# A list scheduler that counts a buffer as free once its store has landed, with another order of the first layer's 29 products

## The chip, the cores and the metric

The kernel runs on one core of one Trainium2 chip. The metric is the device time of one launch in microseconds (us). Before the change it is 998.1 us, the median of three runs.

## What is computed

Sigmoid attention over 8 batches of 12 heads, and then a feed-forward layer with a squared ReLU, all in fp32:

```python
scores = scale * np.matmul(q, k.transpose(0, 1, 3, 2)) - np.log(S)      # q, k, v: (8, 12, 448, 64)
attn = 1.0 / (1.0 + np.exp(-scores))
x = np.matmul(attn, v).transpose(0, 2, 1, 3).reshape(3584, 768)
h = x @ w_in                                                            # 768 -> 2048
r = np.maximum(h, 0.0)
return (s * (r * r) + b) @ w_out                                        # 2048 -> 768
```

## The kernel before

**Stages.** Attention (24 steps) writes x to DRAM. The first 512 of the 3584 tokens then go through the feed-forward layer plainly (the *plain* stage, which the first layer follows at 378.5 us): 16 blocks f, each with a first product into a PSUM tile `ph`, an activation chain r, r*r, s*r+b and a split g on ScalarE and VectorE, and a second product into `po`. The other 3072 tokens go in two groups of three blocks of 512. Each group runs a first layer of 29 products (`LAYERS[0]`: a fast scheme in place of 36 block products) and a second of 15. A product r of the first layer runs as two *units* of 12 matmuls, p = 0 and 1; the first layer of a group has 58 units.

**Precision.** Each fp32 operand is split in two fp32r parts: hi is a copy on ScalarE, lo is the difference on VectorE. An operand `s_14_0l` is the lo part of product 14's operand in group 0, `a_21` a raw block of x, `a_t`, `a_o` sums of such blocks, `h_...` a PSUM bank pair with a product, `G...` a sum of products in SBUF. An entry of `SUMS` for the weights is made on VectorE as `t_f_g` (f is the quarter of the weights, g the group of rows), split, and stored to the DRAM tensors `wd`, from which each unit fetches its 512 KB of weights as `wu`. The sums for later quarters (`t_e`, `t_r`, `t_y`, `t_p`, `t_u`) are made during the first layer.

**Order.** From the plain stage on, each engine's order is made by the list scheduler `Flow.run` (lines 213 to 254) at build time. It takes, of all operations that are able to run, the one with the earliest planned start, and then the earliest due time; PE's order is fixed by `seq`. A transfer out is an SP operation with cost 0.1 and a lag (5 to 9) that counts for those who read what it wrote. The engines run their orders strictly from front to back, SP too: an instruction that waits holds up all behind it. SP's transfers take eight completion semaphores in turn, so a transfer is issued only when the eighth before it has landed.

**Buffers.** `Slots` (line 504) hands out named buffers, the one that was freed first coming first. In the plain stage 13 buffers of 6 KB per partition (c0 to c7, t0 to t4, the list `cx`) hold the weights and the sums `t_f_g`; a sum's buffer is given back in the same step that issues its store, and the next tile in it waits on the chip until that store has landed. The two layers use the list `heap` with buffers of 4 KB. When all of the plain stage is planned, `end` closes its pools and gives `heap` 34 more buffers l0, l1, ..., which lie where c0, c1, ... lay: l0 and the first half of l1 in c0, l4 across c2 and c3. A tile in such a buffer waits for the last use of what lay there, its store included. In the kernel before, c3 is last used by `t_3_5` and c0 by `t_3_0`; l0 goes to `s_23_0l`, and l4 to the fourth tile after it, the sum t10 (`a_t_3838`).

**PSUM.** Four bank pairs take the units in turn. A unit that starts or continues a chain in a pair waits until the sum of the product before it has been read by VectorE or ScalarE.

Of the kernel before, what the change touches and what calls it, by code (L numbers as in the profile page):

```python
# [118 lines left out]
         28: ("o28", "t8", 1)},  # L119
        chains=((14, 5, 25, 0), (4,), (23, 27, 18), (12,), (10, 11, 7, 9, 8), (2,), (22, 16),  # L120
         (15, 3, 19, 24), (13, 17, 28, 21, 1, 26), (20,), (6,)),
        seq=((20, 1), (23, 0), (14, 1), (27, 0), (5, 1), (18, 0), (25, 1), (12, 0), (0, 1), (2, 0),
         (15, 1), (10, 0), (3, 1), (11, 0), (19, 1), (7, 0), (24, 1), (9, 0), (13, 1), (8, 0),
         (17, 1), (22, 0), (28, 1), (16, 0), (21, 1), (4, 0), (1, 1), (6, 0), (26, 1)),
        accs={"00": (("S19", 1), ("S26", 1), ("S3", -1), ("S8", -1)),
         "01": (("S13", 1), ("S19", -1), ("S4", 1)),
         "02": (("S1", 1), ("S10", -1)),
# [36 lines left out]
        seq=((8, 0), (13, 1), (6, 0), (10, 1), (7, 0), (1, 2), (2, 3), (3, 0), (5, 2), (4, 3), (11, 1),  # L164
         (12, 3), (14, 0), (0, 1), (9, 0)),
# [14 lines left out]
    ),  # L180
)

ON_VECTOR = (("13", 1),)
FIRST_RAW = ("20", "11", "12", "21", "22", "10", "00", "02", "01")


class Op:
# [11 lines left out]
class Flow:  # L199
# [13 lines left out]
    def run(self, free):  # L213
        tensor = [o for o in self.ops if o.eng == "PE"]
        t = 0.0
        for o in tensor:
            t += o.cost
            o.due = t
        for o in reversed(self.ops):
            for x, whole in o.next:  # L220
                o.due = min(o.due, x.due - x.cost - (o.lag if whole else -o.cost))
        free = {"PE": 0.0, "DVE": 0.0, "ACT": 0.0, "SP": 0.0, **free}
        able = {e: [o for o in self.ops if o.eng == e and not o.wait] for e in free}
        tensor = tensor[::-1]
        left = len(self.ops)
        while left:
            best = None
            point = tensor[-1].due if tensor else 1e9
            for e, at in free.items():
                for o in able[e]:  # L230
                    if e == "PE" and o is not tensor[-1]:
                        continue
                    need = o.need()
                    if need:
                        far = o.due - o.cost - o.lag - point
                        if far > o.ahead or need + o.heap.spare * (far > self.FAR) > len(o.heap.free_):
                            continue
                    key = (max(at, o.ready), o.due)
                    if best is None or key < best[0]:
                        best = (key, o)  # L240
            (start, _), o = best
            if o.eng == "PE":
                tensor.pop()
            able[o.eng].remove(o)
            o.fn()
            free[o.eng] = start + o.cost
            o.end = start + o.cost + o.lag
            left -= 1
            for x, whole in o.next:
                x.wait -= 1  # L250
                x.ready = max(x.ready, o.end + self.LATENCY if whole else start)
                if not x.wait:
                    able[x.eng].append(x)
        return free
# [213 lines left out]
def sigmoid_attention_relu2_ffn(  # L468
# [11 lines left out]
    B, NQ, P, _, _, S = qk.shape  # L480
    D = v.shape[5]
    NF, _, DM = w_in.shape
# [20 lines left out]

    class Slots:


        def __init__(self, pl, n, tag, ahead=1e9, spare=0):
            self.free_ = [(pl, f"{tag}{i}") for i in range(n)]
            self.at = {}
            self.ahead, self.spare = ahead, spare  # L510

        def more(self, pl, n, tag):
            self.free_ += [(pl, f"{tag}{i}") for i in range(n)]

        def tile(self, shape, dtype, name):
            pl, tag = self.free_.pop(0)
            t = pl.tile(shape, dtype, tag=tag, name=name)
            self.at[id(t)] = (t, pl, tag)
            return t

        def free(self, t):
            _, pl, tag = self.at.pop(id(t))
            self.free_.append((pl, tag))

    heap = Slots(pool(ctx, "h0", 1), 1, "g", 24.0, 4)
    first = ExitStack()
# [22 lines left out]
    def f32(ap):  # L549
        return ap.bitcast(F32)  # L550
# [166 lines left out]
    at = ExitStack()  # L717
# [326 lines left out]
    flow = Flow(heap)  # L1044
# [6 lines left out]
    class Emit:  # L1051
# [101 lines left out]
        def out(self, net, n, k, v):  # L1153
            m, c = self.block[k]
            v.uses += 1
            v.stored = True

            def fn():
                out_store(f32(v.t), KC * c, threes[n][m], KC)
                net.drop(v)  # L1160

            flow.op("SP", 0.1, fn, (v.by,))

        units = []

        def matmuls(self, flow, cost, fn, after, n, l, r, p):
            x = len(self.units)
            rows = made.get((l, p, LAYERS[l]["operand"][r][0]), [])
            old = self.units[x - ROLL] if x >= ROLL else None
            w = flow.op("SP", 0.1, fetch, [old, *rows], lag=5.0, behind=self.ready)  # L1170
            self.ready = [w]
            first = [self.evicted[x - 1]] if 0 < x < 4 else []
            u = flow.op("PE", cost, fn, [w, *after, *first], behind=[self.switch])
            self.units.append(u)
            if 5 <= x < 8:

                def store():
                    out_store(f32(outs[x - 5]), 2 * (x - 5), 0, 2)
                    spare.free(outs[x - 5])
                    heap.free_.append(spare.free_.pop())  # L1180

                flow.op("SP", 0.1, store, (u,))
            return u

    em = Emit()
# [12 lines left out]
    def finish(n, k, p, v, sign):  # L1198
# [3 lines left out]
        s = sign * v.sign  # L1202
        if (k, p) in ON_VECTOR:
            v.by = flow.op(
# [104 lines left out]
    def out_store(src, e, t, n):  # L1309
        dst = out[e * P : (e + n) * P, t * TB : (t + 1) * TB]  # L1310
        nc.sync.dma_start(dst.rearrange("(c p) t -> p c t", p=P), src)
# [265 lines left out]
```

## Time and profile before

| | |
|---|---|
| median of three runs | 998.1 us (997.24, 998.1, 1000.76) |
| the profiled execution's own time | 997.09 us |
| its span | 995.3 us |
| PE busy | 984.9 us (99%) |
| VectorE (DVE) busy | 853.2 us (86%) |
| ScalarE (ACT) busy | 704.0 us (71%) |
| mean DMA rate over the span | 283 GB/s |

The span is the time from the first to the last instruction of one profiled execution; the execution's own time is 1.8 us longer. PE is busy nearly throughout, so what can be won on it is in its few waits, and what can be lost is any new wait. The stages have different limits, and each is read from its own window.

### The profile page before, as it was taken

The numbers are of one execution on the slowest core, as the hardware profiler recorded it, in microseconds if no ns is written. First come the engines' busy times: TensorE is split into PE (matmuls) and PEld (weight loads), VectorE is DVE, ScalarE is ACT, GpSimd is POOL, SyncE is SP. The second block draws the span as 40 slices with busy tenths as digits, with TensorE's granted clock in tenths as the row PEclk, the third lists the DMA queues.
The fourth block names the chain that finished last, engine by engine and source line by source line (L and its number), as shares of the span: only waits on it lengthen the run. The fifth ranks groups of instructions, "written<-read, shape, count | busy, mean of one in ns | idle before, by whom it ended". The sixth has DMA issues, their size and how long they took to land.

```text
span 995.3 us, 13889 instructions
## 1 busy us (share of the span) xinstructions
PE 984.9 (99%) x5240; PEld 774.9 (78%) x5240; DVE 853.2 (86%) x939; ACT 704.0 (71%) x768; POOL 0.2 (0%) x4
## 2 busy tenths in 40 slices
PE   9999999999999989999999999999999999999998
PEld 4545555554888878887888888888888888888887
DVE  5999999997899787998999999975786789999932
ACT  7999999998777566557899945522447799955500
POOL 0000000000000000000000000000000000000000
PEclk9999999999999999999999999999999999999999
DMA  9788989996688999987887677899766676777773
GB/s 328 281 329 345 352 334 370 361 383 249 242 324 346 373 403 399 400 326 272 321 280 231 204 223 252 242 326 318 236 208 199 204 207 197 207 222 247 227 239 123
DMA packets 100210, 281.94 MB, mean 283 GB/s; under 512 B 10160, under 2 KB 20528, under 8 KB 100144
## 3 DMA queue, kind: packets, MB, share of 16 engines
q1 hardware_dynamic: 99856, 280.59, 81.8%
q8 instruction: 42, 0.69, 0.3%
q10 hardware_dynamic: 288, 0.46, 0.1%
q14 instruction: 24, 0.20, 0.0%
HBM read 196.08 MB, written 84.93 MB: 282 GB/s over the span
## 4 chain that ended last, share of the span: by engine, by line
PE 60%; DVE 6%; DMA 3%; ACT 1%; issue 1%; SPq 0%; DVEq 0%; ACTq 0%
PE o L1107 31%; PE h L1107 28%; DVE t L568 2%; DVE w L568 1%; DMA wd<-t 1%; DVE t L565 1%; DMA wd<-t_u 1%; DVE g L568 1%; PE po L1317 1%; DMA a<-xd 1%; ACT s_0h L1086 0%; DMA wu<-wd 0%; SPq L710 0%; PE o L1124 0%; DVE G L565 0%
## 5 line engine op out<-in xcount | busy, mean ns | idle before, releaser
L1107 PE MATMUL h<-s_0h,wu 128*128 128x512 f32 x928 | 276.6, 379 | 1.8 <-DVE G L565 1.8
L1107 PEld LDWEIGHTS h<-s_0h,wu 128*128 128x128 f32 x928 | 175.4, 189 | 27.1 <-DVE G L565 2.2
L1107 PE MATMUL h<-s_0l,wu 128*128 128x512 f32 x464 | 175.9, 379 | 0.0
L773 ACT ACTIVATE a<-psc,nls 128x896 f32<-128x896 f32 x144 | 132.0, 1016 | 10.9 <-PE psc L793 8.7
L827 PE MATMUL pav<-a,v 128*64 128x448 f32 x576 | 113.8, 543 | 1.4
L1107 PEld LDWEIGHTS h<-s_0l,wu 128*128 128x128 f32 x464 | 87.7, 189 | 12.5
L827 PEld LDWEIGHTS pav<-a,v 128*64 128x64 f32 x576 | 39.1, 137 | 65.7 <-issue 45.3
L1200 ACT ACTIVATE G<-G 128x1024 f32<-128x1024 f32 x68 | 69.9, 1049 | 10.0 <-DVE G L565 9.8
L1107 PE MATMUL o<-g_0h,wu 128*128 128x512 f32 x240 | 76.3, 379 | 0.0
L1107 PE MATMUL o<-g_1h,wu 128*128 128x512 f32 x240 | 76.3, 379 | 0.0
L1107 PE MATMUL o<-g_2h,wu 128*128 128x512 f32 x240 | 76.3, 379 | 0.0
L1107 PE MATMUL o<-g_3h,wu 128*128 128x512 f32 x232 | 73.7, 379 | 0.0
L1317 PE MATMUL po<-g,w 128*128 128x512 f32 x288 | 66.9, 387 | 3.1 <-ACT g L1452 2.9
L1317 PEld LDWEIGHTS po<-g,w 128*128 128x128 f32 x288 | 55.5, 193 | 12.3 <-ACT g L1452 3.3
L1080 ACT COPY G<-h 128x1024 f32<-128x1024 f32 x36 | 36.4, 1012 | 36.0 <-PE h L1107 22.3
L936 PE MATMUL ph<-x0h,w 128*128 128x512 f32 x192 | 59.5, 380 | 0.0
L793 PE MATMUL psc<-qkh 64*128 64x448 f32 x282 | 53.8, 378 | 0.0
L565 DVE TENSOR_TENSOR G<-G,h 128x1024 f32<-128x1024 f32 x40 | 48.1, 1213 | 3.8 <-PE h L1107 3.8
L1107 PEld LDWEIGHTS o<-g_0h,wu 128*128 128x128 f32 x240 | 45.4, 189 | 6.5
L1107 PEld LDWEIGHTS o<-g_1h,wu 128*128 128x128 f32 x240 | 45.4, 189 | 6.5
L1107 PEld LDWEIGHTS o<-g_2h,wu 128*128 128x128 f32 x240 | 45.4, 189 | 6.5
L568 DVE TENSOR_TENSOR qkl<-qk,qkh 128x1664 fp32r<-128x1664 f32 (+3 forms) x26 | 44.9, 1726 | 6.3 <-ACT qkh L756 6.1
(222 smaller groups left out, 1978.9 us busy)
## 6 DMA issues: line engine op xcount, KB each, us to landing
wu<-wd SPq DMA_DIRECT2D x236, 512.0 KB, 4.3
wd<-t SPq DMA_DIRECT2D x40, 768.0 KB, 6.3
qk<-qk_t SPq DMA_DIRECT2D x23, 896.0 KB, 7.3
st<-w_out SPq DMA_DIRECT2D x16, 768.0 KB, 9.7
st<-w_in SPq DMA_DIRECT2D x16, 768.0 KB, 8.8
v<-v_t SPq DMA_DIRECT2D x24, 448.0 KB, 5.7
xd<-xo SPq DMA_DIRECT2D x24, 448.0 KB, 4.9
wd<-w SPq DMA_DIRECT2D x16, 512.0 KB, 5.1
```

Of the source, the lines that this page charges most:

```text
L565: nc.vector.tensor_tensor(o, x, y, op=ALU.add)
L568: nc.vector.tensor_tensor(o, x, y, op=ALU.subtract)
L773: nc.scalar.activation(a, psc[:, :, :S], AF.Sigmoid, bias=nls, scale=SCALE)
L793: nc.tensor.matmul(o[:, j, :S], two[wi][r, i, cols], paired(two[xi][r, i, :S]), start=m == 0, stop=m == 2,)
L827: nc.tensor.matmul(pav[r, i, :S], ld_[1][:, 3 * i + c, j, :], a[i, c][:, j, :], start=c == 0, stop=False,)
L936: nc.tensor.matmul(ph, w[:, k, wi, kc * P : (kc + 1) * P], paired(x0[h][xi][:, cc, :]), start=m == 0, stop=m == 3 * NCC - 1,)
L1080: nc.scalar.copy(o, self.view(x, l))
L1107: nc.tensor.matmul(bank.t[0][:, j], wt[:, w, wi, x * P : (x + 1) * P], paired((o.hi, o.lo)[xi][:, c, :]), start=new and m == 0, stop=stop ...
L1200: v.by = flow.op("ACT", cost, lambda: nc.scalar.activation(f32(v.t), f32(v.t), *a, **kw), (v.by,))
L1317: nc.tensor.matmul(pos[e], w[:, k, wi, kc * P : (kc + 1) * P], paired(g[:, gi, :]), start=first and i == 0, stop=last and i == 2,)
```

## The change

The scheduler's planned start now includes the time at which the buffers that an operation would take come free (`Slots.ready`), and a buffer given back by an operation comes free at that operation's planned end with its lag (`Slots.now`). The two kinds of output stores get lags of 8 and 9. The buffers that `more` adds come with the free time 0. The first layer's units run in another order; which products are chained in a bank is as before. Two more of the 24 squared ReLUs of a group go from two ScalarE instructions to one VectorE instruction: three in place of one. `FIRST_RAW` is read nowhere.

```diff
-        seq=((20, 1), (23, 0), (14, 1), (27, 0), (5, 1), (18, 0), (25, 1), (12, 0), (0, 1), (2, 0),
...
+        seq=((12, 1), (14, 0), (23, 1), (5, 0), (27, 1), (25, 0), (18, 1), (0, 0), (20, 1), (15, 0),
...
-ON_VECTOR = (("13", 1),)
+ON_VECTOR = (("01", 0), ("12", 0), ("20", 0))
...
-                    key = (max(at, o.ready), o.due)
+                    key = (max(at, o.ready, o.heap.ready(need)), o.due)
                     if best is None or key < best[0]:
                         best = (key, o)
             (start, _), o = best
             if o.eng == "PE":
                 tensor.pop()
             able[o.eng].remove(o)
+            free[o.eng] = start + o.cost
+            type(o.heap).now = o.end = start + o.cost + o.lag
             o.fn()
-            free[o.eng] = start + o.cost
-            o.end = start + o.cost + o.lag
...
     class Slots:
 
+        now = 0.0
 
         def __init__(self, pl, n, tag, ahead=1e9, spare=0):
-            self.free_ = [(pl, f"{tag}{i}") for i in range(n)]
+            self.free_ = [(pl, f"{tag}{i}", 0.0) for i in range(n)]
...
         def more(self, pl, n, tag):
-            self.free_ += [(pl, f"{tag}{i}") for i in range(n)]
+            self.free_ += [(pl, f"{tag}{i}", 0.0) for i in range(n)]
+
+        def ready(self, n):
+            return max((x[2] for x in self.free_[:n]), default=0.0)
 
         def tile(self, shape, dtype, name):
-            pl, tag = self.free_.pop(0)
+            pl, tag, _ = self.free_.pop(0)
...
         def free(self, t):
             _, pl, tag = self.at.pop(id(t))
-            self.free_.append((pl, tag))
+            self.free_.append((pl, tag, self.now))
...
-            flow.op("SP", 0.1, fn, (v.by,))
+            flow.op("SP", 0.1, fn, (v.by,), lag=8.0)
...
-                flow.op("SP", 0.1, store, (u,))
+                flow.op("SP", 0.1, store, (u,), lag=9.0)
```

What this moves on VectorE where `t_3_2` takes its buffer, late in the plain stage. Before (the buffer is that of `t_2_6`, whose lo part is the first row):

```order
L568 TENSOR_TENSOR t_2_6_3436<-t_2_6_3436 128x3x256
L565 TENSOR_TENSOR t_3_0_3463<-wf_15_2682 128x256
L568 TENSOR_TENSOR t_3_0_3463<-wf_7_2681,t_3_0_3463 128x256
L568 TENSOR_TENSOR t_3_0_3463<-t_3_0_3463 128x256
L568 TENSOR_TENSOR w_6_3519<-wf_6_125,w_6_3519 128x3x256
L568 TENSOR_TENSOR t_2_3_3374<-t_2_3_3374 128x3x256
L568 TENSOR_TENSOR t_2_4_3400<-t_2_4_3400 128x3x256
L568 TENSOR_TENSOR t_3_1_3537<-wf_3_114,wf_11_116 128x256
L568 TENSOR_TENSOR t_3_2_3561<-wf_3_114,wf_11_116 128x256
```

On the same engine and at the same place, now (the buffer of `t_3_2` is that of `t_2_3`, whose lo part stands six rows ahead of the first row):

```order
L572 TENSOR_TENSOR g_3463<-r_3428,g_3463 128x512
L572 TENSOR_TENSOR t_2_6_3471<-wf_6_126,wf_10_112 128x256
L572 TENSOR_TENSOR w_7_3466<-wf_7_2681,w_7_3466 128x3x256
L569 TENSOR_TENSOR t_2_6_3471<-wf_10_112 128x256
L569 TENSOR_TENSOR t_2_6_3471<-wf_2_110 128x256
L572 TENSOR_TENSOR t_2_5_3438<-t_2_5_3438 128x3x256
L572 TENSOR_TENSOR w_6_3517<-wf_6_125,w_6_3517 128x3x256
L572 TENSOR_TENSOR t_3_0_3524<-wf_7_2681,wf_15_2682 128x256
L572 TENSOR_TENSOR t_2_6_3471<-t_2_6_3471 128x3x256
L572 TENSOR_TENSOR t_3_1_3530<-wf_3_114,wf_11_116 128x256
L572 TENSOR_TENSOR t_3_2_3533<-wf_3_114,wf_11_116 128x256
```

The new tile stood seven VectorE instructions behind the one whose store it waits for; it now stands fifteen behind.

VectorE at the end of the plain stage and the start of the first layer, before (`g` is the last activation split, after which `s_23_0l` takes l0):

```order
L568 TENSOR_TENSOR t_3_5_3670<-t_3_5_3670 128x3x256
L568 TENSOR_TENSOR g_3746<-r_3731,g_3746 128x512
L568 TENSOR_TENSOR s_23_0l<-a_o_3735,s_23_0h 128x1024
L568 TENSOR_TENSOR a_t_3832<-a_11_3478,a_21_3486 128x1024
L568 TENSOR_TENSOR a_t_3834<-a_20_3475,a_22_3521 128x1024
L568 TENSOR_TENSOR a_t_3836<-a_12_3481,a_t_3832 128x1024
L565 TENSOR_TENSOR a_t_3838<-a_t_3836,a_t_3834 128x1024
L568 TENSOR_TENSOR a_o_3840<-a_22_3521,a_t_3836 128x1024
L565 TENSOR_TENSOR a_t_3834<-a_21_3486,a_t_3834 128x1024
L568 TENSOR_TENSOR s_14_0l<-a_21_3486,s_14_0h 128x1024
```

The same place now:

```order
L572 TENSOR_TENSOR t_3_5_3673<-t_3_5_3673 128x3x256
L572 TENSOR_TENSOR g_3751<-r_3743,g_3751 128x512
L572 TENSOR_TENSOR s_14_0l<-a_21_3487,s_14_0h 128x1024
L572 TENSOR_TENSOR a_o_3833<-a_11_3492,a_12_3495 128x1024
L572 TENSOR_TENSOR a_t_3835<-a_11_3492,a_21_3487 128x1024
L572 TENSOR_TENSOR a_t_3837<-a_20_3557,a_22_3705 128x1024
L572 TENSOR_TENSOR a_t_3839<-a_12_3495,a_t_3835 128x1024
L569 TENSOR_TENSOR a_t_3841<-a_t_3839,a_t_3837 128x1024
L572 TENSOR_TENSOR a_o_3843<-a_22_3705,a_t_3839 128x1024
L569 TENSOR_TENSOR a_t_3837<-a_21_3487,a_t_3837 128x1024
L572 TENSOR_TENSOR s_23_0l<-a_o_3833,s_23_0h 128x1024
```

Product 14 is now the second product (units 2 and 3) and 23 the third (units 4 and 5). `s_14_0l` takes l0, the first tile after the plain stage; in the changed plan c0, where l0 lies, is last used by `t_3_5`.

SP's queue at the same place, before (`wd<-` rows are stores of weight sums and weights, `wu` fetches for units; the program's first fetch for a unit and five raw blocks stand further ahead):

```order
L698 DMA wd_3_96<-w_7_3631 128x2x512
L698 DMA wd_3_96<-w_15_3660 128x3x512
L1427 DMA wd_1_92<-t_3_0_3463 128x3x512
L1427 DMA wd_1_92<-t_3_6_3674 128x3x512
L1038 DMA wu_0_20_1_3729<-wd_1_92 128x1024
L1038 DMA wu_0_23_0_3733<-wd_0_91 128x1024
L1427 DMA wd_1_92<-t_3_3_3597 128x3x512
L1427 DMA wd_1_92<-t_3_4_3636 128x3x512
L1427 DMA wd_1_92<-t_3_5_3670 128x3x512
```

SP's queue now (two fetches for units and five raw blocks, a_10 among them, stand further ahead; the sixth, a_22, is here):

```order
L1042 DMA wu_0_14_0_3661<-wd_0_91 128x1024
L1042 DMA wu_0_14_1_3665<-wd_1_92 128x1024
L1042 DMA wu_0_23_0_3668<-wd_0_91 128x1024
L1431 DMA wd_1_92<-t_3_0_3524 128x3x512
L1431 DMA wd_1_92<-t_3_2_3533 128x3x512
L714 DMA a_22_3705<-xd_86 128x2x256
L714 DMA a_22_3705<-xd_87 128x2x256
L1431 DMA wd_1_92<-t_3_4_3630 128x3x512
L702 DMA wd_3_96<-w_15_3709 128x3x512
L1431 DMA wd_1_92<-t_3_6_3677 128x3x512
L1431 DMA wd_1_92<-t_3_3_3595 128x3x512
L1431 DMA wd_1_92<-t_3_5_3673 128x3x512
```

Ahead of the last store of the plain stage, that of `t_3_5`, there are now five fetches for units where there were three, and six raw blocks where there were five; all stores are as many as before.

## Rows read from the trace of the kernel before

**Rows 1.** The waits of PE over the whole span (engine, line, what it waited for: us in total, times, longest).

```profile
PE po L1317 <- ACT g L1452: 2.9, 1, 2.9
PE h L1107 <- DVE G L565: 1.8, 1, 1.8
```

**Rows 2.** The timeline of PE at the end of the plain stage (start us, us, line, operation, out<-in, count; in brackets the idle time before it and its releaser).

```profile
361.23 8.25 PE L1317 MATMUL po<-g,w 128*128 128x512 f32 x36
372.33 0.48 PE L1317 MATMUL po<-g,w 128*128 128x512 f32 x1 [2.85 <-ACT g L1452]
373.06 5.62 PE L1317 MATMUL po<-g,w 128*128 128x512 f32 x17 [0.24 <-DVE g L568]
378.52 0.38 PE L1107 MATMUL h<-s_0h,wu 128*128 128x512 f32 x1
```

**Rows 3.** Busy time of each engine in stretches of the span (PE, PEld, DVE, ACT, POOL, each with its count; then the granted clock as a share of 2.4 GHz, the DMA share and GB/s).

```profile
373.00:378.70 5.70, 5.64 (x18) 4.69 (x19) 4.54 (x5) 2.93 (x5) 0.00 (x0) 0.70 0.99 363
378.70:433.00 54.30, 54.30 (x253) 47.54 (x253) 49.45 (x54) 30.47 (x35) 0.00 (x0) 1.00 1.04 405
458.00:531.00 73.00, 72.80 (x337) 63.79 (x338) 69.39 (x76) 64.37 (x69) 0.00 (x0) 1.00 0.83 283
```

**Rows 4.** The timeline of VectorE around its longest wait in the plain stage, and below it two of the waits in the stretch 283 to 470 us.

```profile
341.18 0.42 DVE L568 TENSOR_TENSOR t<-wf,wf 128x256 f32<-128x256 f32 x1
350.27 0.43 DVE L568 TENSOR_TENSOR t<-wf,wf 128x256 f32<-128x256 f32 x1 [8.67 <-DMA wd<-t]
369.75 1.82 DVE L568 TENSOR_TENSOR t<-t 128x768 fp32r<-128x768 f32 x2
...
DVE w L568 <- ACT w L682: 1.8, 1, 1.8
ACT w L682 <- DMA wd<-t: 1.8, 1, 1.8
```

**Rows 5.** The timeline of ScalarE at the end of the last activation chain.

```profile
366.90 0.59 ACT L1448 ACTIVATE r<-ph 128x512 f32<-128x512 f32 x1
...
369.87 1.04 ACT L1086 CAST s_0h<-a_o 128x1024 fp32r<-128x1024 f32 x1 [1.71 <-DVE a_o L568]
...
371.66 0.62 ACT L1452 CAST g<-r 128x512 fp32r<-128x512 f32 x1
```

**Rows 6.** The timeline of VectorE at the start of the first layer; the row at 386.40 is `s_14_0l`.

```profile
376.32 1.22 DVE L568 TENSOR_TENSOR a_t<-a,a_t 128x1024 f32<-128x1024 f32 x1
382.99 1.23 DVE L565 TENSOR_TENSOR a_t<-a_t,a_t 128x1024 f32<-128x1024 f32 x1 [5.45 <-DMA wd<-t]
...
386.40 1.22 DVE L568 TENSOR_TENSOR s_0l<-a,s_0h 128x1024 fp32r<-128x1024 f32 x1
```

**Rows 7.** The last three stores of the plain stage, those of `t_3_3`, `t_3_4` and `t_3_5`: the transfers of `wd` issued in two short stretches (count, ns of the issue, first and last start), with their times from issue to landing.

```profile
L1427 SPq DMA_DIRECT2D wd<-t x2: 371/410/450, 369.9 to 370.7; - x2
DMA to landing us min/median/max: 9.1/9.9/10.6
...
L1427 SPq DMA_DIRECT2D wd<-t x1: 360/360/360, 371.6 to 371.6; - x1
DMA to landing us min/median/max: 11.3/11.3/11.3
```

**Rows 8.** Stretches of the span with the columns of rows 3, from the start of the heavy storing to the landing of the last store.

```profile
285.00:309.00 24.00, 24.00 (x112) 21.00 (x112) 23.97 (x46) 18.44 (x28) 0.00 (x0) 1.00 1.05 408
309.00:315.00 6.00, 6.00 (x29) 5.27 (x28) 4.20 (x10) 4.23 (x7) 0.00 (x0) 1.00 0.93 357
315.00:320.00 5.00, 5.00 (x24) 4.37 (x24) 5.00 (x11) 3.95 (x7) 0.00 (x0) 1.00 0.42 163
320.00:335.00 15.00, 15.00 (x71) 13.14 (x70) 14.86 (x30) 10.96 (x18) 0.00 (x0) 1.00 1.05 408
335.00:346.00 11.00, 11.00 (x53) 9.63 (x52) 6.60 (x11) 6.75 (x11) 0.00 (x0) 1.00 1.01 329
...
350.00:370.00 20.00, 19.43 (x89) 16.36 (x87) 19.73 (x36) 14.87 (x22) 0.00 (x0) 1.00 1.05 407
370.00:375.00 5.00, 2.43 (x6) 1.77 (x7) 4.26 (x5) 2.83 (x4) 0.00 (x0) 0.82 0.98 343
375.00:383.00 8.00, 8.00 (x35) 6.86 (x34) 2.55 (x4) 3.88 (x6) 0.00 (x0) 0.90 1.05 413
```

**Rows 9.** DMA issues of the whole span (out<-in, queue, count, KB each, median us from issue to landing).

```profile
wu<-wd SPq DMA_DIRECT2D x236, 512.0 KB, 4.3
wd<-t SPq DMA_DIRECT2D x40, 768.0 KB, 6.3
```

**Rows 10.** The timelines of VectorE and of PE at PE's other wait.

```profile
451.07 1.22 DVE L568 TENSOR_TENSOR s_0l<-a,s_0h 128x1024 fp32r<-128x1024 f32 x1
455.18 0.69 DVE L568 TENSOR_TENSOR t_e<-wr 128x512 f32<-128x512 f32 x1 [2.89 <-DMA wd<-t_u]
...
458.20 0.48 PE L1107 MATMUL h<-s_0h,wu 128*128 128x512 f32 x1 [1.82 <-DVE G L565]
```

**Rows 11.** The squared ReLU on either engine: the instructions of line 1206, and a group of the page's part 5.

```profile
L1206 DVE SCALAR_TENSOR_TENSOR G<-G x2: 1211/1214/1218, 545.1 to 822.4; 128x1024 f32<-128x1024 f32 x2
...
L1200 ACT ACTIVATE G<-G 128x1024 f32<-128x1024 f32 x68 | 69.9, 1049 | 10.0 <-DVE G L565 9.8
```

More of the change, by code (lines that the diff above doesn't have):

```diff
@@ L121 @@
          (15, 3, 19, 24), (13, 17, 28, 21, 1, 26), (20,), (6,)),
-        seq=((20, 1), (23, 0), (14, 1), (27, 0), (5, 1), (18, 0), (25, 1), (12, 0), (0, 1), (2, 0),
-         (15, 1), (10, 0), (3, 1), (11, 0), (19, 1), (7, 0), (24, 1), (9, 0), (13, 1), (8, 0),
-         (17, 1), (22, 0), (28, 1), (16, 0), (21, 1), (4, 0), (1, 1), (6, 0), (26, 1)),
+        seq=((12, 1), (14, 0), (23, 1), (5, 0), (27, 1), (25, 0), (18, 1), (0, 0), (20, 1), (15, 0),
+         (22, 1), (3, 0), (16, 1), (19, 0), (4, 1), (24, 0), (2, 1), (10, 0), (13, 1), (11, 0),
+         (17, 1), (7, 0), (28, 1), (9, 0), (21, 1), (8, 0), (1, 1), (6, 0), (26, 1)),
         accs={"00": (("S19", 1), ("S26", 1), ("S3", -1), ("S8", -1)),
@@ L181 @@
 )
-ON_VECTOR = (("13", 1),)
-FIRST_RAW = ("20", "11", "12", "21", "22", "10", "00", "02", "01")
+ON_VECTOR = (("01", 0), ("12", 0), ("20", 0))
+FIRST_RAW = ("10", "21", "11", "12", "20", "22", "01", "02", "00")
 class Op:
```

## The prediction

> **What bounds the kernel now.** I read first the waits of PE over the whole span. There are two that matter: 2.9 us for the last activation split, and 1.8 us for a sum on VectorE [rows 1]. PE does the same matmuls after the change, so a gain can come from these two places alone, and a loss only from a new wait.
>
> The timeline shows the first place. PE ends 36 matmuls at 361.23 + 8.25 = 369.48, waits 2.85, then 0.24, and the remaining 17 take 5.62 at a granted clock of 0.70 on average, so partly at 1.2 GHz [rows 2, 3]. At full clock 253 matmuls start in 54.30 us, 0.215 each [rows 3]; the last 18 would have ended 18 x 0.215 = 3.9 after 369.3, and the first layer would start at 373.2, not at 378.52 [rows 2]. This place costs 5.3 us.
>
> Its cause is on VectorE: nothing runs for 8.67 us, behind a store's landing [rows 4], and the order shows why: `t_3_2` takes the buffer of `t_2_6` seven instructions after the latter's last use. ScalarE's chain then ends late, held up once more by 1.71 [rows 5]. The second place is of one kind with it: `t_e` waits 2.89 for the landing of `t_u`'s store, and the sum that PE needs stands behind it; PE loses 1.82 [rows 10].
>
> **The change, part by part.** *The planned waits.* Both cases are what the new key sees. `t_3_2` now stands 15 instructions behind its store. Without the 8.67 us, the last `t` lo ends not at 371.6 [rows 4] but near 363; the last split cannot come before the last `ph` at 361.2 plus four ScalarE steps and one on VectorE, some 365 to 367 (two such steps take 0.6 each, [rows 5]), still ahead of 369.3. So PE would reach the first layer at 373.2: -5.3 us there. `t_e` should lose its wait too: -1.8 us.
>
> *What is late next.* I follow l0. `s_14_0l`, needed by unit 2, now takes l0, which lies in c0; c0's last user is now `t_3_5`, whose store is the last of the plain stage. Buffers from `more` have free time 0, so the plan does not know of this wait. Before, the same wait fell on l4 (the 5.45 at 382.99, [rows 6]), when `s_23_0l` and three sums were already done. Call the landing of that store R. Before: issued 371.6, 11.3 later landed, R = 382.9 [rows 7], as VectorE's restart at 382.99 shows.
>
> R is set by the DMA, not by VectorE. From 285 us on the DMA share is 1.05 at 407 or 408 GB/s in all stretches but 309 to 320, 335 to 346 (share 1.01, raw blocks moving at 329) and 370 to 375 [rows 8]. All that SP issues ahead of the last store must pass first. Now there are two more unit fetches and one more raw block ahead, 3 x 512 KB (a fetch in [rows 9]; a raw block is 128 x 1024 fp32, the same size): 1.57 MB / 408 GB/s = 3.9 us. Raw blocks are slower: (408 - 329) GB/s x 11 us = 0.87 MB lost over the five of them, 0.4 us for one. Sum 4.3. Against it, gaps that can close: 309 to 315, (408 - 357) x 6 = 0.31 MB, 0.7 us; 315 to 320, 245 x 5 = 1.2 MB, 3.0 us; 370 to 375, 0.8 us [rows 8]. The first two follow a wait of the removed kind (ScalarE's split waits 1.8 for a store, VectorE 1.8 for the split, [rows 4]); I count them as closed. R = 382.9 + 4.3 - 3.7 = 383.5; bounds 382.7 (all closed) and 387.2 (none).
>
> Then PE: units 0 and 1 run from 373.2 to 373.2 + 24 x 0.215 = 378.4. Unit 2 waits for `s_14_0l`, R + 1.1 = 384.6: a new wait of 6 us. Unit 4 needs `s_23_0l`, ninth on VectorE after R; one instruction takes (386.40 - 382.99) / 3 = 1.14 [rows 6], so R + 10.3 = 393.8, a second new wait of 2 to 4 us. Before, unit 4 began at 378.52 + 48 x 0.215 = 388.8. So the hand-over comes out at 393.8 - 388.8 = +5.0 us, not -5.3. Before, 17 matmuls after a wait of 2.85 took 5.62, where 3.7 were due: 1.9 for the clock [rows 2, 3]. After unit 2's wait this is covered, since unit 4 waits anyway; after unit 4's it costs 0 to 1.9. The wait of 1.82 [rows 10] stands in no low clock. I take 1.0.
>
> *VectorE for ScalarE.* Four more VectorE instructions of 1.21 in all, eight fewer of 1.05 on ScalarE [rows 11]: 2.4 us on VectorE in each group's first layer. Between 458 and 531 VectorE has 73.0 - 69.4 = 3.6 us free [rows 3], which hides it; uncovered it costs 2.4. No gain: PE waits for ScalarE nowhere but at the hand-over. I take 0.
>
> *The order of products* has no price of its own beyond what it puts in l0. New lags of output stores only affect later buffer choice: 0.
>
> Sum: +5.0 + 1.0 - 1.8 = +4.2 us on 997.1, so 1001.3. The median of the runs lies 1.0 above the profiled execution; 1002 on that basis, +0.4%. 0.5% (5 us) is about what a measurement of this kernel can tell from no change, so this counts as no change, near the edge.
>
> **The rivals.** *The gain arrives.* If R does not wait for all that stands ahead, both PE waits go and nothing replaces them: -5.3 - 1.8 = -7.1, 991. With a landing of 6.3, the median of such stores [rows 9], after an issue at 364 to 366, R is 370 to 372, earlier than unit 2 can ask. It breaks even (clock apart) at R + 10.3 = 388.8 + 1.8, R = 380.3. Against it: the last three stores took 9.1, 10.6 and 11.3, each landing behind the one before [rows 7], and the DMA has no room [rows 8]. The Trainium skill says otherwise in principle: its page "DMA: Bandwidth & Descriptors", section "Queues, rings and completion order", says that completion is not first-in, first-out per issuing engine. By that rule the last store could overtake and this rival would hold, 991; the order of the landings above does not bear it out.
>
> *Slower.* The gaps do not close, since VectorE now waits elsewhere for the crowded DMA: R = 387.2, unit 4 at 397.5, +8.7; the full 1.9 for the clock; -1.8: +8.8, 1006 to 1007. The total is R - 380.3 plus the clock's part: it passes 5 us at R = 385.3 with none of it and at 383.4 with all. For it: SP issues raw blocks in a burst, and the store of `t_2_5` stands behind eight such transfers. Against: the cause of the biggest gap is gone.
>
> *It does not do what it says.* The plan's SP steps cost 0.1 and landings vary from 4 to 11, so waits of the old kind come back and the stall before the hand-over stays in part; with the wait on l0 behind it, that is 1000 +- 3, since R, not the stall, then sets the start.
>
> **How the numbers follow.** Forecast 0.52, of which 0.12 ends above +5 us by the clock; gain 0.13, of which 0.01 ends within 5 us; slower 0.28; no effect 0.07. Faster: 0.12. Slower: 0.28 + 0.12 = 0.40. Within: 0.40 + 0.01 + 0.07 = 0.48. Range: from 995, which leaves out most of the gain case, to 1008, above the slower one; the forecast's own range is 998 to 1006.
>
> **What would show it.** Right: the wait for ACT g at `po` is gone and the first matmul of the first layer starts near 373; PE waits some 6 us on VectorE one product later, and again before the third; VectorE waits on `wd<-t` right before its first 128x1024 split after the last g; the DMA gap at 315 to 320 is filled; no wait of `t_e` on `t_u`. The forecast is wrong if VectorE restarts before 380 (faster) or after 385 (slower), or if a PE wait stands after the first ten units.

## The result, and the profile after

| | before | after |
|---|---|---|
| median of six runs | 997.67 us (996.74 to 1000.76) | 1003.48 us (1002.96 to 1004.39) |
| profiled execution, own time and span | 997.09, 995.3 us | 1003.71, 1001.9 us |

After over before: 1.0055, 95% interval 1.004 to 1.007. The waits of PE over the span, after:

```profile
PE h L1111 <- DVE s_0l L572: 8.0, 2, 5.9
PE h L1111 <- DVE a_t L569: 1.1, 1, 1.1
...
PE h L1111 <- DMA wu<-wd: 0.3, 1, 0.3
```

Both waits of [rows 1] are gone; two waits for `s_0l` and two small ones took their place. PE's timeline shows where:

```profile
361.59 11.82 PE L1321 MATMUL po<-g,w 128*128 128x512 f32 x54
...
384.68 0.79 PE L1111 MATMUL h<-s_0l,wu 128*128 128x512 f32 x1 [5.88 <-DVE s_0l L572]
...
393.89 0.48 PE L1111 MATMUL h<-s_0l,wu 128*128 128x512 f32 x1 [2.09 <-DVE s_0l L572]
...
424.45 0.45 PE L1111 MATMUL h<-s_0h,wu 128*128 128x512 f32 x1 [0.33 <-DMA wu<-wd]
...
428.35 0.45 PE L1111 MATMUL h<-s_0h,wu 128*128 128x512 f32 x1 [1.07 <-DVE a_t L569]
```

The 54 matmuls of the plain stage now run without the stall of [rows 2]. PE then stops ahead of unit 2 and of unit 4. VectorE's timeline gives the reason:

```profile
365.62 0.69 DVE L572 TENSOR_TENSOR g<-r,g 128x512 fp32r<-128x512 f32 x1 [0.72 <-ACT g L1456]
383.40 1.22 DVE L572 TENSOR_TENSOR s_0l<-a,s_0h 128x1024 fp32r<-128x1024 f32 x1 [17.09 <-DMA wd<-t]
...
392.62 1.22 DVE L572 TENSOR_TENSOR s_0l<-a_o,s_0h 128x1024 fp32r<-128x1024 f32 x1
...
427.14 1.22 DVE L569 TENSOR_TENSOR a_t<-a,a_t 128x1024 f32<-128x1024 f32 x1 [5.04 <-DMA a<-xd]
```

`s_14_0l` stands 17.09 us behind the landing of a store. In [rows 6] a wait of this kind was 5.45 us, and the operands that PE took first were ahead of it. Stretches of the span (columns of [rows 3]):

```profile
309.00:315.00 6.00, 6.00 (x30) 5.26 (x29) 6.00 (x13) 4.29 (x7) 0.00 (x0) 1.00 1.05 404
315.00:320.00 5.00, 5.00 (x25) 4.39 (x24) 5.00 (x12) 4.93 (x8) 0.00 (x0) 1.00 1.05 406
320.00:335.00 15.00, 15.00 (x71) 13.16 (x70) 13.92 (x25) 10.93 (x17) 0.00 (x0) 1.00 0.95 370
...
370.00:375.00 5.00, 5.00 (x25) 4.38 (x24) 0.00 (x0) 3.52 (x6) 0.00 (x0) 1.00 1.06 402
...
393.90:400.00 6.10, 6.10 (x20) 5.07 (x21) 6.10 (x6) 4.88 (x7) 0.00 (x0) 0.72 0.28 80
```

The DMA gaps of [rows 8] at 309 to 320 and at 370 are filled; a smaller one has opened at 320 to 335. Behind unit 4's wait 20 matmuls take 6.10 us where 20 x 0.215 = 4.3 were due, at a mean granted clock of 0.72: 1.8 us.

Added up: unit 4 at 393.89 against 388.8 is +5.1, the clock +1.8, the waits at 424 and 428 +1.4, the wait of [rows 10] -1.8. That is +6.5; the spans differ by 6.6. The clock's 1.8 and the wait of 0.33 at 424.45 are one item, not two: in the runs l0_last and old_relu below, which have the same hand-over, no low clock followed unit 4 (28 matmuls in about 6.1 us, at 1.00), and PE then waited 1.97 and 1.76 for the same weights, up to 424.47 and 424.34. So about 2 us are lost up to 424 with the low clock or without it, and the landing of those weights sets them.

### The profile page after: what moved, and what is told of

The parts are those of the page before. It is cut to its first block, busy times and chain, and to the rows that moved or that the text cites. A ratio compares the mean times of both kernels' runs of the same rounds, so it can differ in the third digit from the quotient of the medians.

```text
span 1001.9 us, 13890 instructions
## 1 busy us (share of the span) xinstructions
PE 987.1 (99%) x5240; PEld 777.0 (78%) x5240; DVE 857.9 (86%) x943; ACT 692.2 (69%) x756; POOL 0.2 (0%) x4
## 4 chain that ended last, share of the span: by engine, by line
PE 80%; ACT 8%; DMA 5%; DVE 3%; issue 2%; SPq 1%; ACTq 0%; DVEq 0%
PE o L1111 31%; PE h L1111 27%; PE pav L831 9%; ACT a L777 5%; PE ph L940 4%; PE po L1321 3%; DMA wd<-t 2%; PE psc_l L818 2%; PE pav L840 2%; PE psc L797 2%; DMA a<-xd 1%; DVE t L572 1%; DMA out_t<-o 1%; ACT wf L597 1%; DMA wu<-wd 1%
## 5 line engine op out<-in xcount | busy, mean ns | idle before, releaser
L1111 PE MATMUL h<-s_0h,wu 128*128 128x512 f32 x928 | 279.5, 382 | 1.4 <-DVE a_t L569 1.1
L1204 ACT ACTIVATE G<-G 128x1024 f32<-128x1024 f32 x66 | 67.6, 1048 | 27.3 <-DVE G L569 27.0
L1321 PE MATMUL po<-g,w 128*128 128x512 f32 x288 | 64.4, 379 | 0.0
L1084 ACT COPY G<-h 128x1024 f32<-128x1024 f32 x32 | 32.0, 1010 | 32.8 <-PE h L1111 20.8
```

Source lines behind the costliest of these rows:

```text
L1084: nc.scalar.copy(o, self.view(x, l))
L1111: nc.tensor.matmul(bank.t[0][:, j], wt[:, w, wi, x * P : (x + 1) * P], paired((o.hi, o.lo)[xi][:, c, :]), start=new and m == 0, stop=stop ...
L1204: v.by = flow.op("ACT", cost, lambda: nc.scalar.activation(f32(v.t), f32(v.t), *a, **kw), (v.by,))
L1321: nc.tensor.matmul(pos[e], w[:, k, wi, kc * P : (kc + 1) * P], paired(g[:, gi, :]), start=first and i == 0, stop=last and i == 2,)
```

## The experiments

All are compared with the kernel before, timed beside each. The theory was that the loss is where `s_14_0l` lies: in c0, behind the last store. The main rival was that the three more transfers ahead of the hand-over are the loss, whatever waits for them.

**1. l0_last.** Hand out l0 and l1 last, by name.

```diff
             heap.more(pool(ctx, "h2", 1), 34, "l")
+            heap.free_.sort(key=lambda x: x[1] in ("l0", "l1"))
```

> Edit: the changed kernel, with the buffers l0 and l1 (those that lie in c0, which t_3_5 leaves last) put at the end of the list that `more` adds; every engine's order stays as it is, only addresses move. Buffer theory (the loss is that s_14_0l stands behind the landing of t_3_5's store, R = 383.4): VectorE's wait of 17.1 us goes, PE enters the first layer at 373.2 and unit 2 follows without the 5.9 us, unit 4 without the 2.1 us; the first layer is up to 388.8 - 383.6 = 5.3 us earlier than in the kernel before, and the 1.8 us of t_e stay away: 991, or up to 995 if unit weights, which come behind R, are late for units 5 to 7 (due 386 to 391). DMA theory (the three more transfers ahead of the hand-over are the loss, whatever waits for them): the wait moves to the unit weights or the raw block a_22, and the time stays within 2 us of 1003.5.

Measured: 1004.83 us, ratio 1.0086 (1.0069 to 1.0103), VectorE at 383.38 as in the changed kernel. It decides nothing on the theory: a name gets its address at its first use, so `s_14_0l` took l2 and the address was c0 again. It repeats the changed kernel.

**2. c0_last.** The same, but l0 and l1 get their addresses first, by a tile each (`place_0`, `place_1`) that nobody uses, and are then handed out last. The instruction orders are those of the changed kernel.

```diff
-            heap.more(pool(ctx, "h2", 1), 34, "l")
+            pl = pool(ctx, "h2", 1)
+            for i in range(2):
+                pl.tile([P, 2, TB], F32, tag=f"l{i}", name=f"place_{i}")
+            heap.more(pl, 34, "l")
+            heap.free_ = heap.free_[2:] + heap.free_[:2]
```

> Edit: the changed kernel, but the addresses of l0 and l1 (the two buffers in c0) are set aside first and the two are handed out last; every engine's order is that of the changed kernel. s_14_0l now takes a buffer whose last reader is PE, done at 361. Buffer theory: VectorE goes on at 366 without the wait of 17.1 us, waits for the raw block a_22 (near 374) instead, and has s_23_0l near 381; unit 2 and unit 4 follow without a wait, from 373.2 on, 10.3 us ahead of the changed kernel and 5.2 ahead of the kernel before, with no low clock behind a wait: 990 to 993, or up to 996 if the weights of units 5 to 7 (due 386 to 391) are late. DMA theory: the wait moves to the weights or to a_22, and the time stays above 1000.

Measured: 993.15 us (992.82 to 993.66), ratio 0.9955 (0.994 to 0.997): faster than both kernels. VectorE and PE:

```profile
366.27 1.22 DVE L572 TENSOR_TENSOR s_0l<-a,s_0h 128x1024 fp32r<-128x1024 f32 x1
...
373.75 1.23 DVE L572 TENSOR_TENSOR a_t<-a,a 128x1024 f32<-128x1024 f32 x1 [3.99 <-DMA a<-xd]
...
379.56 1.22 DVE L572 TENSOR_TENSOR s_0l<-a_o,s_0h 128x1024 fp32r<-128x1024 f32 x1
```

```profile
413.53 0.45 PE L1111 MATMUL h<-s_0h,wu 128*128 128x512 f32 x1 [1.29 <-DMA wu<-wd]
417.44 0.45 PE L1111 MATMUL h<-s_0h,wu 128*128 128x512 f32 x1 [1.08 <-DVE a_t L569]
```

The raw block a_22 is the next to be late, as expected, and costs PE nothing. PE has no wait from 361 to 413 and so no low clock. The span is 10.9 us shorter than after: 10.3 at unit 4 and 1.8 of clock, less 1.0 at the weights (11.1 by this sum). Measured at the end of the wait for weights it is 424.45 - 413.53 = 10.9. The rival falls.

**3. fetch_late and twice.** These test the bytes ahead of the last store: three fetches behind it, or two more transfers ahead of it. `em.tail` collects the stores of the last quarter.

```diff
-            w = flow.op("SP", 0.1, fetch, [old, *rows], lag=5.0, behind=self.ready)
+            w = flow.op("SP", 0.1, fetch, [old, *rows], lag=5.0, behind=self.ready + (self.tail if x == 2 else []))
...
+                if f == 3:
+                    em.tail.append(o)
```

```diff
+                    if f == 3 and g in (3, 4):
+                        x = dram.tile([P, len(rows) * 2 * KW], F32, name=f"twice_{g}")
+                        nc.sync.dma_start(x, f32(box[0]).rearrange("p k h c -> p (k h c)"))
                     stored.update((0, f, n) for n in rows)
```

> Edit: the changed kernel with the fetches of weights for units 2 to 4 (3 x 512 KB) held behind the last store of the plain stage; t_3_5 still leaves c0 last and s_14_0l still takes l0. The term of the prediction (R falls by 1.57 MB / 408 GB/s = 3.9 us): VectorE restarts at 379.5 instead of 383.4, unit 4 starts at 389.8 instead of 393.9, and the time falls by 4: 999 to 1000, if the weights of unit 2, now 1.3 us behind R, are not much later than s_14_0l. Rival (R hangs on VectorE, ScalarE or on when SP issues the last store, not on the bytes ahead of it): R stays above 382 and the time at 1002 to 1005.

> Edit: the changed kernel with two more transfers of 768 KB out of the buffers of t_3_4 and t_3_3 to a scratch tensor, ahead of the last store (1.57 MB that nobody reads). By the same term R rises by 3.9 us to 387.3, unit 4 starts at 397.8 and the time rises by 3.9 to 1007.5, by 3.4 to 5 with the clock. Rival (the landing hangs on something else): 1003 to 1005.

Measured: fetch_late 999.71 us, ratio 1.0027 (1.0016 to 1.0038); twice 1007.71, ratio 1.0103 (1.0086 to 1.012). `s_14_0l` on VectorE and unit 4 on PE, first of fetch_late, then of twice:

```profile
379.14 1.22 DVE L572 TENSOR_TENSOR s_0l<-a,s_0h 128x1024 fp32r<-128x1024 f32 x1 [13.37 <-DMA wd<-t]
...
389.63 0.48 PE L1111 MATMUL h<-s_0l,wu 128*128 128x512 f32 x1 [2.19 <-DVE s_0l L572]
```

```profile
388.54 1.22 DVE L572 TENSOR_TENSOR s_0l<-a,s_0h 128x1024 fp32r<-128x1024 f32 x1 [21.49 <-DMA wd<-t]
...
399.03 0.48 PE L1111 MATMUL h<-s_0l,wu 128*128 128x512 f32 x1 [1.36 <-DVE s_0l L572]
```

R moves by -4.3 and +5.1 where 3.9 were due, unit 4 with it by -4.3 and +5.1, and the medians by -3.8 and +4.2. The term holds in size, within 0.4 and 1.2 us. In twice the plain stage's last g on VectorE starts 0.7 later than after (366.36 against 365.62), in fetch_late 0.5 earlier (365.08). That these shifts make up the difference is not shown: in l0_last that g starts 0.8 earlier (364.79), and R stays at 383.38.

What the bytes move is the issue of the last store. The last stores on SP's queue, of fetch_late, after and twice in turn (ns of the issue, first and last start, then the times to landing):

```profile
L1431 SPq DMA_DIRECT2D wd<-t x2: 1097/1367/1637, 365.3 to 366.5; - x2
DMA to landing us min/median/max: 11.6/12.0/12.5
L1431 SPq DMA_DIRECT2D wd<-t x1: 1852/1852/1852, 371.4 to 371.4; - x1
DMA to landing us min/median/max: 11.9/11.9/11.9
L1431 SPq DMA_DIRECT2D wd<-t x1: 770/770/770, 376.5 to 376.5; - x1
DMA to landing us min/median/max: 11.9/11.9/11.9
```

The last store goes out at 366.5, 371.4 and 376.5 and lands 12.5, 11.9 and 11.9 later. So the time behind the issue stays nearly the same, and the added bytes hold up the queue ahead of it.

**4. sched_alone and order_alone.** Each half of the change by itself (the old order with the new scheduler; the new order with the old scheduler). The choice of squared ReLUs goes with the order.

```diff
-        seq=((12, 1), (14, 0), (23, 1), (5, 0), (27, 1), (25, 0), (18, 1), (0, 0), (20, 1), (15, 0),
...
+        seq=((20, 1), (23, 0), (14, 1), (27, 0), (5, 1), (18, 0), (25, 1), (12, 0), (0, 1), (2, 0),
...
-ON_VECTOR = (("01", 0), ("12", 0), ("20", 0))
+ON_VECTOR = (("13", 1),)
```

This is sched_alone, from the changed kernel; order_alone is the reverse edit of the kernel before.

> Edit: the changed kernel with the old order of the products and the old choice of squared ReLUs; the scheduler's new key and the lags stay. Here c0 is last used by w_7, whose store stands far ahead of the last; t_3_5 lies in c7, under l10 and l11 (a raw block and s_14_0h). Buffer theory: the stall before the hand-over goes (-5.3 us), t_e's wait too (-1.8 us), and the first operands after the hand-over wait for no late store; third product's hi needs t_3_5's landing near 380, its unit is due at 383.6, so 0 to 2 us of new wait, and up to 3 us if the weights of the fourth unit, fetched behind t_3_5's store, are late: 991 to 996, faster than the kernel before. Rival (a plan that waits for landings is itself the loss, since it moves fetches ahead of stores): 1001 to 1004.

> Edit: the kernel before with the new order of the products and the new choice of squared ReLUs; the scheduler is the old one. c0 is now last used by t_3_2, whose store stands three stores (5.8 us of DMA time) ahead of that of t_3_5; VectorE's order at the hand-over is that of the changed kernel. Buffer theory: VectorE restarts near 377.6, unit 2 waits 0.4 to 1 us, unit 4 starts near 388 in place of 388.8 before: with 0 to 1.9 us for the clock and 0 to -1.8 us for t_e the time is 995 to 999. Rival (the order of the products is the loss, since it sets the fetches ahead of the stores): 1002 to 1005, as the changed kernel.

Measured: sched_alone 998.39 us, ratio 1.0008 (0.9999 to 1.0018); order_alone 1000.88, ratio 1.0042 (1.0027 to 1.0057). Both missed their ranges by 2 us, for reasons beyond the hand-over. There both did as expected: sched_alone has no wait of PE up to 447, and in order_alone VectorE and PE show

```profile
376.61 1.23 DVE L568 TENSOR_TENSOR s_0l<-a,s_0h 128x1024 fp32r<-128x1024 f32 x1 [8.98 <-DMA wd<-t]
```

```profile
361.27 11.82 PE L1317 MATMUL po<-g,w 128*128 128x512 f32 x54
372.92 0.38 PE L1107 MATMUL h<-s_0h,wu 128*128 128x512 f32 x1
...
387.10 0.52 PE L1107 MATMUL h<-s_0l,wu 128*128 128x512 f32 x1 [2.19 <-DVE s_0l L568]
...
418.99 0.45 PE L1107 MATMUL h<-s_0h,wu 128*128 128x512 f32 x1 [1.66 <-DMA wu<-wd]
```

so unit 4 starts 1.7 us earlier than before (388.8). The first two rows of PE show more: with the old scheduler the stall ahead of the hand-over is gone as well (VectorE's longest wait for a store in the plain stage is 3.44 us here, 8.67 before), and so is the wait at 458. The new order is enough for that, as the new scheduler is in sched_alone. The later waits (1.66, and 2.6 from 487 to 521) and the clock behind unit 4 (in the stretch 384.7 to 393.9, 25 matmuls take 7.00 us, 1.6 too long) give back more: -1.7 - 1.8 + 1.66 + 2.6 + 1.6 = +2.4, of the 3.4 by which the spans differ; 1.0 stays unexplained. In sched_alone one wait at 452 takes the whole gain:

```profile
452.14 0.79 PE L1111 MATMUL h<-s_0h,wu 128*128 128x512 f32 x1 [5.04 <-ACT G L1084]
```

```profile
430.00:458.00 28.00, 22.89 (x94) 18.85 (x93) 19.96 (x21) 20.56 (x22) 0.00 (x0) 0.88 0.71 250
```

The second row is its stretch 430 to 458: beside the 5.04, 94 matmuls take 22.89 where 20.2 were due, 2.7 for the clock. 7.7 lost against 7.1 gained is 998.

**5. order_late_last and before_c3_last.** The edit of c0_last (with 12 addresses given out first) with the buffers in c0 and c3 on order_alone, and with those in c3 alone (l4, l5) on the kernel before.

```diff
+            heap.free_.sort(key=lambda x: x[1] in ("l0", "l1", "l4", "l5"))
```

> Edit: the run order_alone with the buffers that lie in c0 and c3 (l0, l1, l4 and l5; t_3_2 and t_3_4 leave them last) handed out last; every order stays. Buffer theory: VectorE's wait of 9.0 us goes, and with it PE's waits of 1.0 and 2.2 us at 384 and 387 and the 1.7 us of half clock behind them: 1000.9 - 4.9 = 996, 993.5 to 997.5 with the waits that stay (1.7 us for weights at 419, four of 0.5 to 0.8 near 490 and 520). Rival (the new order of the products without the scheduler is bad beyond the hand-over): 999 to 1001.

> Edit: the kernel before, with the two buffers that lie in c3 (l4 and l5; t_3_5 leaves c3 last) handed out last; every order stays. VectorE's wait of 5.45 us at 382.99 goes, but in the kernel before no operand that PE takes soon stands behind it, and PE enters the first layer at 378.5 because of the stall ahead of the hand-over, which stays. Buffer theory: 997 within 1.5 us, as the kernel before. Rival (what counts is when VectorE gets going again, whoever waits): 5 us earlier, 991 to 994.

Measured: order_late_last 996.22 us, ratio 0.9986 (0.9974 to 0.9997), 4.7 below order_alone; before_c3_last 997.03, ratio 0.9984 (0.9974 to 0.9994). Both as expected. Freeing VectorE 5 us earlier gains next to nothing in the kernel before, since nobody waits for it there:

```profile
PE po L1317 <- ACT g L1452: 2.9, 1, 2.9
PE h L1107 <- DVE G L565: 1.0, 1, 1.0
```

**6. sums_lag and sched_late_last.** Two tries at the wait at 452 of sched_alone: a longer lag for the stores of the later sums, or late buffers last.

```diff
-            o = flow.op("SP", 0.1, store, by[:1], late=due, lag=9.0)
+            o = flow.op("SP", 0.1, store, by[:1], late=due, lag=16.0)
```

```diff
+            heap.free_.sort(key=lambda x: x[1] in ("l4", "l5", "l10", "l11"))
```

> Edit: the run sched_alone (new scheduler, old order of the products and old choice of squared ReLUs) with the lag of the stores of the later sums at 16 in place of 9. In sched_alone the hand-over had no wait and the gain of 7 us was lost at 452 us, in a wait of 5.0 us for ScalarE and 6.8 us of half clock behind it. Theory A: it was lost because ScalarE waited 5.1 us at 424 for t_e's store, whose buffer a copy of a bank takes; with the larger lag the copy takes another buffer, the wait at 452 goes and the time is 990 to 993. Theory B: VectorE has too little time left between 373 and 450 once PE starts 5 us earlier, and the loss comes back as another wait for VectorE or ScalarE: 996 to 999.

> Edit: the run sched_alone with the buffers that lie in c3 and c7 (l4, l5, l10 and l11; t_3_6 and t_3_5 leave them last) handed out last; every order stays. There VectorE lost 1.8 and 3.8 us after the hand-over behind these stores. Theory B (VectorE falls behind a PE that starts 5 us earlier, and PE's wait of 5.0 us at 452 with the low clock behind it is that lag): the 5.6 us are given back to VectorE, the wait at 452 goes or shrinks, 990 to 994. Theory C (the wait at 452 is set by ScalarE's own order, a copy of a bank behind seven squared-ReLU instructions): the wait stays, 996 to 999.

Measured: sums_lag 1006.83 us, ratio 1.0093 (1.0077 to 1.0109), outside both ranges: the other plan has three waits of PE (5.30 at 439, 4.22 at 489, 3.09 at 536). Theory A's forecast fails, and why that plan is so much worse stays open. Since the whole plan changed, this run alone does not refute theory A; sched_relu below speaks against it. sched_late_last 998.11, ratio 0.9996 (0.9983 to 1.0008): VectorE has `s_14_0l` at 375.00 in place of 380.50, and PE still waits 5.04 at 452, so theory B falls too.

**7. old_relu and sched_relu.** The choice of squared ReLUs, undone in the changed kernel, and kept in sched_alone. The line of `ON_VECTOR` is the only difference from the changed kernel and from sched_alone.

> Edit: the changed kernel with the old choice of squared ReLUs for VectorE (one a group in place of three). In its plan t_3_5 lies in c0 as before. Buffer theory: the two waits of 5.9 and 2.1 us stay, 1003.5 within 1.5 us; the small wait of 1.1 us near 427 may change. Rival (the VectorE work added is the loss): 1.2 x 4 = 4.8 us less VectorE work, and the time falls by 2 to 5 us, to 999 to 1001.

> Edit: the changed kernel with the old order of the products alone (new scheduler, new choice of squared ReLUs). As in sched_alone, no late store stands ahead of the first operands. On ScalarE the copy of the bank for which PE waited 5.0 us at 452 in sched_alone now stands ahead of the three squared-ReLU instructions that were in front of it, and the copy of the second bank still stands behind some. Theory C (that wait is set by ScalarE's order): the wait shrinks to 0 to 3 us, the low clock behind it goes or shrinks, 990 to 995. Rival (VectorE has too little time there, and gets 1.2 us of work more for each of the two squared ReLUs): 998 to 1001.

Measured: old_relu 1004.31 us, ratio 1.0075 (1.006 to 1.009), as the changed kernel. sched_relu 994.72, ratio 0.9968 (0.9956 to 0.998). ScalarE and PE in sched_alone, then in sched_relu:

```profile
447.13 1.99 ACT L1204 ACTIVATE G_t<-G_t 128x1024 f32<-128x1024 f32 x2
449.02 1.23 ACT L1204 ACTIVATE G_t<-G_t,b_sb,s_sb 128x1024 f32<-128x1024 f32 x1
450.15 1.04 ACT L1204 ACTIVATE G_t<-G_t 128x1024 f32<-128x1024 f32 x1
451.10 1.90 ACT L1084 COPY G<-h 128x1024 f32<-128x1024 f32 x2
```

```profile
424.25 1.02 ACT L1084 COPY G<-h 128x1024 f32<-128x1024 f32 x1 [5.14 <-DMA wd<-t_e]
...
444.74 1.00 ACT L1084 COPY G<-h 128x1024 f32<-128x1024 f32 x1
...
451.05 0.99 ACT L1084 COPY G<-h 128x1024 f32<-128x1024 f32 x1
```

```profile
452.10 0.59 PE L1111 MATMUL h<-s_0h,wu 128*128 128x512 f32 x1 [2.55 <-ACT G L1084]
```

The first of the two copies now comes at 444.74, PE goes on one unit (2.6 us) longer and waits 2.55 for the second. ScalarE's wait of theory A is still there (5.14 us for the store of `t_e`, at 424), so it does not set PE's wait by itself. What PE waits for is a copy that stands late in ScalarE's order (theory C). The edit also takes two squared ReLUs off ScalarE, and no run tells the copy's place from this lighter load.

The hand-over in one view (PE enters the first layer between 372.6 and 373.9 in all but the kernel before, where it is 378.5):

| kernel | who leaves c0 last | `s_14_0l` starts on VectorE | unit 4 starts on PE | median, us |
|---|---|---|---|---|
| before | t_3_0 (t_3_5 leaves c3) | 386.40, needed third | 388.8 | 997 |
| sched_alone | w_7 | 380.50, needed third | no wait | 998.4 |
| order_alone | t_3_2 | 376.61 | 387.10 | 1000.9 |
| fetch_late | t_3_5, three fetches fewer ahead | 379.14 | 389.63 | 999.7 |
| after | t_3_5 | 383.40 | 393.89 | 1003.5 |
| twice | t_3_5, two transfers more ahead | 388.54 | 399.03 | 1007.7 |
| c0_last | t_3_5, c0 handed out last | 366.27 | no wait | 993.2 |
| order_late_last | t_3_2, c0 and c3 handed out last | 367.35 | no wait | 996.2 |

## Why the prediction came out as it did

- **The planned waits.** Right in what goes and in size: PE entered the first layer at 373.2, and the wait of [rows 10] is gone. That the new key is what removes them is shown only for the old order (sched_alone); order_alone lost both waits without the key.
- **What is late next.** Right in mechanism and size: R = 383.40 (forecast 383.5), unit 2 at 384.68 (384.6), unit 4 at 393.89 (393.8). c0_last shows that the wait is the address alone: same orders, same transfers, 10 us less. fetch_late and twice show the byte term, which acts by a later issue of the last store.
- **The gaps.** Those at 309 to 320 closed as counted. Not foreseen: 320 to 335 lost (408 - 370) x 15 = 0.57 MB, 1.4 us, and the gap at 370, left out of the sum, closed: 0.7 us. Over the whole of 285 to 383 the DMA moved 393 GB/s where it had moved 380, 1.3 MB more against the 1.57 MB that were added. The size of the main step is right; that R came out within 0.1 us is in part luck, since errors of up to 1.4 us offset each other.
- **The clock.** 1.0 was mis-sized: 1.8, near the end of its range. But the end does not hang on it: l0_last and old_relu have no low clock there and reach the unit at 424 no earlier, since its weights land no earlier.
- **VectorE for ScalarE.** 0 holds here (old_relu). It is not 0 in general: with the old order it is worth 998.39 - 994.72 = 3.7 us. There it was ScalarE that PE waited for, behind the hand-over, which the prediction had not looked for.
- **Order of products.** Counted at 0 beyond l0. The two waits at 424 and 428, 1.4 us, are the part of the sum that was missing, and by the prediction's own sign (a PE wait after the first ten units) this part of it failed. At full clock the first of them is about 2 us (l0_last, old_relu), so the weights of that unit are the larger item. The one of 1.07 or 1.08 stands in fetch_late, twice and c0_last too, so it is no result of the hand-over but of this plan (a raw block that lands late, 5.04 on VectorE). Neither wait was taken apart further.

The two misses together, 0.8 + 1.4, take the profiled execution from the forecast 1001.3 to 1003.5; it measured 1003.71. The median, 1003.48, did not lie 1.0 above that execution, as the forecast of 1002 had taken it to; this second error hid part of the first. The result is just over the 0.5% that was to count as no change. The rival "the gain arrives" needed a landing that does not wait for what stands ahead. The runs show R moving with the bytes ahead of it. The Trainium skill's page "DMA: Bandwidth & Descriptors" (section "Queues, rings and completion order") says that completion is not first-in, first-out per issuing engine. No overtaking is seen here: in the trace after, all transfers that SP issued between 358 and 384 us landed in the order of their issue, at 402 to 410 GB/s from 350 to 383. The page's rule did not help this rival.

## What to carry to other kernels

A planner that prices a buffer by its landing should carry that price through every hand-over of memory: here one list of 34 buffers with free time 0 let the first operand take the latest buffer, and a gain of 4 us (c0_last) became a loss of 6. No run gave the 34 buffers their true free times; c0_last moved two addresses by hand. When a stall is removed, ask which wait it was covering and what takes the late buffer first; the address of two buffers was worth 10.3 us (c0_last against after), while c0_last and sched_relu, with the two orders of the 29 products and no late buffer ahead of the first operands, differ by 1.6. In a list with 1% of slack on PE, judge each part of a change beside the others: the new scheduler alone gave +1 us, which its interval does not tell from nothing, with the new squared ReLUs -3, the whole change with two addresses moved -4.

## What the runs showed that was not expected

A wait of PE can cost more than itself, as the prediction had it; not expected was that its length does not say whether it will. Behind those of 2.09 us (after), 5.04 (sched_alone) and 2.55 (sched_relu) the granted clock was at its half level, 1.2 GHz, for a stretch, which cost 1.8 us in the first and 2.7 in the second. c0_last ran through waits of 1.29 and 1.08 at a mean granted clock of 1.00, but so did twice behind a wait of 2.22 (at 430) and sums_lag behind one of 3.09 (at 536). And low clock can be free: after lost 1.8 us to it and, as l0_last and old_relu show, would otherwise have waited nearly as long for weights. Plans are also fragile: one number, the lag of some stores, moved the time by 8 us (sums_lag against sched_alone).
